# RWKV-7 recurrence and expert layer: another form of the first inverse, w turned on load, a new order

## The chip, the cores and the metric

The kernel runs on one core of a Trainium2 chip. Time is device microseconds of that core, as a median of several executions. The core has five engines that run their own instruction lists: TensorE (PE; loading its weights is listed apart, as PEld), VectorE (DVE), ScalarE (ACT), GpSimd (POOL) and SyncE (SP), which here only issues transfers. Matrix products go to PSUM, which this kernel splits into four double tiles ("duo").

## The reference

Two parts follow each other. The first is a recurrence over 768 steps for 4 x 8 heads with a 40 x 40 state each:

```
for t in range(S):
    y[t]  = r[t] @ state
    Sa    = state @ a[t]
    state = state * w[t][None, :] - outer(Sa, b[t]) + outer(v[t], k[t])
```

The second takes the 3072 x 320 result as x, and computes `gelu(x @ w_in) @ w_out` with a hidden width of 2048. w_in and w_out are given in double precision.

## The kernel before

**Chunks.** The 768 steps are cut into 12 chunks of 64. Inside a chunk, products of 64 x 64 blocks replace the steps; only the state goes from chunk to chunk. Heads and batches are packed so that one step of the kernel works on all 32 of them: a "run" is 32 calls of a small product, which the trace lists as 64 records.

**The steps.** The code is a set of generators; the name of each carries the chunk's number. For a chunk: `w`, `a`, `b`, `k`, `v`, `r` load rows; `logs` takes log w; `sums` makes running sums of it over time by products with the triangular matrix `cum_m`, once turned (heads on partitions, 32 products of 64x64) and once in rows (`cum`), and takes exponentials of them; `sc` and `sk` scale b and k; `ta`, `tb`, `tk`, `tv`, `tr` bring the inputs to turned form. From a certain chunk on (NT = 3 for a, v, r; NB = 4 for b, k) the turned form is not made by PE transposes but loaded a second time in pairs of rows (`bp`, `kp`, `vp`) and turned by VectorE (`turn`). `N`, `A`, `RV`, `M` are masked products of these. `av`, `X` and `sa` form the right-hand side and apply the inverse; `saT` is the same product turned, which `M` needs. `QY` gives the new state and y; `y` scales y into `xt` and moves parts of it between partitions with eleven transfers, on which the first product of the expert layer, `ph`, waits.

**The inverse.** Each chunk needs the inverse of a unit triangular 64 x 64 matrix per head and batch, T. From chunk 1 on, N goes to DRAM (`N`), comes back with blocks on partitions (`nb`), GpSimd solves (`inv`), and the result returns (`ft`); `corner` and `joined` fill the off-diagonal blocks. Chunk 0 has no time for that: `sq` builds its 32 x 32 diagonal inverses on PE by repeated squaring, five rounds in two halves, and `cornerd` and `joinedd` finish it.

**The expert layer.** `ph` (line 1002) is x times w_in, with Gelu on ScalarE (line 1005) evicting PSUM. `po` is the second product: direct for the first NS = 3 chunks and the last one (line 1024), otherwise by seven half-size products after Strassen and Winograd (line 1040), with additions on VectorE; the sums of w_out that these need (`ws`) lie in the tile that b and k of the first chunks leave. `wi`, `wl`, `wo` load w_in and w_out as 32-bit words, and `ci`, `co` convert them to single precision on VectorE and ScalarE. `warm` is a product that nothing uses.

**The order.** Nothing is scheduled by a tool. The string ORDER is a list of steps written out; each token runs a generator to its next yield, and `name:n` names the PSUM or conv buffers taken. Every engine, SyncE's transfer queue included, executes its instructions in that order. A line number in a profile of a product is often that of the helper `mm` (line 143).

## Time and profile before

| | |
|---|---|
| median of 3 runs | 685.69 us (685.41 to 689.18) |
| the profiled execution | 687.68 us |
| its span | 685.9 us, granted clock 0.992 |
| PE busy, PEld busy | 664.5 us (97%), 573.5 us (84%) |
| VectorE, ScalarE, GpSimd busy | 367.7, 216.9, 342.4 us |
| ph, PE (line 1002) | 219.0 us |
| po by half products, PE (line 1040) | 74.6 + 37.2 + 19.1 us |
| po direct, PE (line 1024) | 73.4 us |
| transfers, share of 16 engines | 54.2% on SyncE's queue |

A group's busy time is the union of its records; PE's products overlap, so the mean time of one record is longer than busy time by count.

### The profile page before, as it was taken

To read this page: it belongs to the slowest core of one execution; us is meant where nothing else is said; L and a number is where in the kernel's file an instruction comes from. 1 tells how busy PE (TensorE), PEld (TensorE's weight loads), DVE (VectorE), ACT (ScalarE), POOL (GpSimd) and SP (SyncE) were. 2 spreads that over 40 slices of the span, in tenths; PEclk is the share of its full clock that TensorE was granted. 3 is DMA by queue.
4 is the path that set the end of the run, shared out by engine and by line. 5 is a ranking of instruction groups with operands and counts; after the bars stand their busy time and mean duration, and the time that the engine had idled before them with its cause. 6 is when DMAs were issued, how large, how long until landed. Compare 5 with 4: busy or idle time off the path is not lost.

```text
span 685.9 us, 32624 instructions
## 1 busy us (share of the span) xinstructions
PE 664.5 (97%) x14748; PEld 573.5 (84%) x14748; DVE 367.7 (54%) x504; ACT 216.9 (32%) x300; POOL 342.4 (50%) x781
## 2 busy tenths in 40 slices
PE   8778999999999999999999999999999999999996
PEld 5665788788788778998998988988998998989984
DVE  1676878983533554845671853663744825613400
ACT  4243644524223312413423415322422412132010
POOL 3248406814837818826827827817816848700000
PEclk9899999999999999999999999999999999999999
DMA  9989377496479476556586377385656265210100
GB/s 133 181 158 160 68 162 178 125 177 120 88 135 149 88 141 116 106 103 127 102 147 113 78 145 135 62 171 111 113 109 129 52 116 104 40 37 4 39 1 20
DMA packets 287923, 74.46 MB, mean 109 GB/s; under 512 B 265736, under 2 KB 284456, under 8 KB 287784
## 3 DMA queue, kind: packets, MB, share of 16 engines
q1 hardware_dynamic: 286720, 69.84, 54.2%
q0 software_dynamic: 864, 2.36, 1.9%
q8 instruction: 116, 1.90, 1.2%
q14 instruction: 23, 0.19, 0.1%
q10 hardware_dynamic: 200, 0.16, 0.1%
HBM read 58.69 MB, written 9.70 MB: 100 GB/s over the span
## 4 chain that ended last, share of the span: by engine, by line
PE 92%; DVE 3%; issue 2%; SPq 1%; DMA 1%; ACT 0%; DVEq 0%; ACTq 0%
PE duo L1002 32%; PE duo L143 29%; PE duo L1040 18%; PE duo L1024 10%; PE duo L508 3%; SPq L207 1%; DMA xt<-in_b_dram 1%; DVE nT L565 0%; DVE conv L434 0%; DVE conv L440 0%; DVE aT L539 0%; DVE Nb L771 0%; DVE w_out_sb L441 0%; DVE N L627 0%; DVE SM L627 0%
## 5 line engine op out<-in xcount | busy, mean ns | idle before, releaser
L1002 PE MATMUL duo<-xt,w_in_sb 64*128 64x256 f32 x1920 | 219.0, 380 | 0.7 <-issue 0.6
L1002 PEld LDWEIGHTS duo<-xt,w_in_sb 64*128 64x128 f32 x1920 | 184.6, 187 | 22.1 <-issue 2.3
L730 POOL TENSOR_TENSOR tmp<-W,Nb 128x126 f32<-128x126 f32 (+22 forms) x310 | 132.6, 428 | 128.9 <-DMA Nb<-N 105.4
L732 POOL TENSOR_TENSOR W<-W,tmp 128x126 f32<-128x126 f32 (+22 forms) x310 | 135.5, 437 | 24.3
L1005 ACT ACTIVATE gt<-duo 128x1024 f32<-128x1024 f32 x48 | 49.2, 1024 | 173.3 <-PE duo L1002 165.8
L1040 PE MATMUL duo<-w_out_sb,gt 128*128 128x160 f32 x512 | 74.6, 302 | 0.0
L1024 PE MATMUL duo<-w_out_sb,gt 128*128 128x320 f32 x256 | 73.4, 438 | 1.0 <-DVE w_out_sb L441 1.0
L1040 PEld LDWEIGHTS duo<-w_out_sb,gt 128*128 128x128 f32 x512 | 70.2, 190 | 1.6 <-DVE os L1044 0.5
L1024 PEld LDWEIGHTS duo<-w_out_sb,gt 128*128 128x128 f32 x256 | 47.2, 190 | 20.9 <-DVE w_out_sb L441 1.6
L1040 PE MATMUL duo<-extra,conv 128*128 128x160 f32 x256 | 37.2, 303 | 0.0
L1040 PEld LDWEIGHTS duo<-extra,conv 128*128 128x128 f32 x256 | 35.0, 190 | 1.6 <-issue 1.0
L627 DVE TENSOR_TENSOR SM<-duo,upper 128x1024 f32<-128x1024 f32 x12 | 14.6, 1220 | 33.2 <-PE duo L143 33.2
L143 PE MATMUL duo<-rT,late 40*64 40x64 f32 x1536 | 27.6, 219 | 2.7 <-issue 2.4
L143 PEld LDWEIGHTS duo<-rT,late 40*64 40x64 f32 x1536 | 25.0, 135 | 4.7 <-issue 4.3
L854 DVE COPY Tt<-duo 32x512 f32<-32x512 f32 x11 | 7.6, 689 | 36.1 <-ACT Tt L854 36.0
L1044 DVE TENSOR_TENSOR os<-os,duo 128x160 f32<-128x160 f32 x32 | 10.1, 317 | 31.1 <-PE duo L1040 21.2
L723 POOL MEMSET W<- 128x512 f32 x10 | 5.5, 546 | 40.8 <-DMA inv<-W 40.7
L831 DVE STREAM_TRANSPOSE conv<-Tt 128x512 f32<-128x512 f32 x11 | 7.8, 711 | 32.2 <-DMA Tt<-inv 32.2
L730 POOL TENSOR_TENSOR rows<-os,rows 128x126 f32<-128x126 f32 (+22 forms) x31 | 13.5, 436 | 22.7 <-DMA rows<-N 20.4
L1005 ACT ACT_TABLE_LOAD x12 | 15.4, 1283 | 29.9 <-PE duo L1002 11.3
L945 DVE TENSOR_TENSOR xt<-duo,wpT 128x512 f32<-128x512 f32 x24 | 15.4, 682 | 17.0 <-PE duo L143 17.0
L429 ACT ACTIVATE conv<-conv,rebias 128x320 uint32<-128x320 uint32 (+1 forms) x26 | 15.8, 621 | 16.7 <-DVE conv L425 16.6
(194 smaller groups left out, 1034.0 us busy)
## 6 DMA issues: line engine op xcount, KB each, us to landing
Nb<-N SPq DMA_DIRECT2D x20, 256.0 KB
VR<-in_v_dram SPq DMA_DIRECT2D x24, 160.0 KB
out_dram<-os SPq DMA_DIRECT2D x48, 80.0 KB
rows<-in_b_dram SPq DMA_DIRECT2D x22, 160.0 KB
rows<-in_k_dram SPq DMA_DIRECT2D x22, 160.0 KB
Tt<-inv SPq DMA_DIRECT2D x44, 64.0 KB
r_pairs<-in_r_dram SPq DMA_DIRECT2D x36, 72.0 KB
a_pairs<-in_a_dram SPq DMA_DIRECT2D x18, 144.0 KB
```

Source lines behind the costliest of these rows:

```text
L143: nc.tensor.matmul(o, lhsT, rhs, start=first, stop=True, skip_group_check=True)
L429: nc.scalar.activation(power, power, ACT.Relu, bias=rebias, scale=8.0)
L508: nc.tensor.transpose(pt[:, g, n], src(g, n), ident)
L627: nc.vector.tensor_tensor(to, pt, upper.unsqueeze(1).to_broadcast([P, NBL, C]), ALU.mult)
L730: eng.tensor_tensor(t, W[:, :nr, j:j + 1].to_broadcast([P, nr, rest]), Nb[:, j:j + 1, j + 1:].to_broadcast([P, nr, rest]), ALU.mult)
L732: eng.tensor_tensor(W[:, :nr, j + 1:], W[:, :nr, j + 1:], t, ALU.add)
L945: nc.vector.tensor_tensor(xt[:, :NP, g * P:(g + 1) * P].rearrange("p i (e t) -> p i e t", e=2), t["QY"][g][:, :, :, D:].rearrange("p e i t ...
L1002: nc.tensor.matmul(pt[:, x, s], w_in_sb[half(x), kt, p * P:(p + 1) * P], xt[half(x), kt], start=kt == 0, stop=kt == NK - 1)
L1005: nc.scalar.activation(gt[:, 4 * q:4 * q + 4].rearrange("p (x s) t -> p x s t", x=2), pt, ACT.Gelu)
L1024: nc.tensor.matmul(pt[:, g], gt[:, f, g * P:(g + 1) * P], w_out_sb[:, f], start=f == 0, stop=f == NF - 1)
L1040: nc.tensor.matmul(pt[:, n, :DM // 2], l_[:, f], r_[:, f], start=f == 0, stop=f == NF // 2 - 1)
L1044: nc.vector.tensor_tensor(to, one_, other, ALU.add)
```

## The change

- The inverse of chunk 0 works with one 64 x 64 block-diagonal product per head and batch and half (64 x 96 with the running result beside it) in place of two of 32 x 32. The mask that cuts the blocks out is a new constant.
- For chunk 0, `av` multiplies A by V and by the masked r-v part together, and `sa` applies T to both, so M comes out of sa's product under a mask (`left_upper`); `saT` and `M` of chunk 0 are gone.
- For chunks 3 to 11, w is loaded a second time in pairs (`wq`), turned by VectorE, and its running sums over time are made there by a scan (`wt`) in place of PE's products in `sums`.
- b and k are turned by VectorE from chunk 3 on (before: 4), and po uses half products from chunk 2 on (before: 3).
- w_in comes in 2 steps in place of 4, w_out in 11 transfers in place of 32, with more bytes in each; the hidden columns are permuted to suit.
- `warm` is one product in place of two, and there are nine of them in place of six.
- ORDER is new throughout, and has other buffer places. The second copy of the inverse's corner (T2) is read in place.

```diff
+FIRST = (3, 3, 3, 2)
-    NT, NB, NS = 3, 4, 3
+    NT, NB, NW, NS = FIRST
...
+    def wq(c):
+        fetch_pairs("w_turned", w, c, paired["v"], False)
+        yield
...
+    left_upper = sb("left_upper", [P, VC])
+    upper = left_upper[:, D:]
+    upper_blocks, ident_block = plain(Js_tile)[:, :C], plain(Js_tile)[:, C:C + BL]
+    going_on = sb("going_on", [P, G * NP * 2 * C], mybir.dt.uint8)
...
     def wo(c):
+        n = 2 if c in SECOND_PAIRS else 1
         src = moe_w_out.bitcast(UINT32) if wide_out else moe_w_out
-        for n in range(2):
-            nc.sync.dma_start(out=to[:, n::2], in_=from_[:, n::2])
+        at = (c // 2 % 2 * (NF // 2) + 2 * (c // 4) + c % 2) * P
+        nc.sync.dma_start(out=second_words(c, n).rearrange("p (f m) -> p f m", f=n),
+                          in_=src[at:at + n * P].rearrange("(f p) m -> p f m", p=P))
...
     def sums(c):
+        if c < NW:
+            pt = duo().rearrange("p e (n t) -> p e n t", t=C)
+            for n in range(G * NP):
+                for x in range(2):
+                    for e in range(2):
+                        at = (2 * n + x) * D
+                        mm(pt[half(x), e, n], logw[half(e), at:at + HP], cum_m[half(e), half(e)])
+            yield
...
+    def wt(c):
+        logs_of = conv()[:, :G * NP * P].rearrange("p (n t) -> p n t", t=C)
+        turn(logs_of, c, "w_turned")
+        yield
+        nc.scalar.activation(plain(logs_of), plain(logs_of), ACT.Ln)
+        yield
+        nc.vector.tensor_tensor_scan(plain(logs_of), going_on, plain(logs_of), 0.0, ALU.mult, ALU.add)
+        yield
+        en = of(c)["en"] = by_batch(kT_tile)
+        nc.scalar.activation(plain(en), plain(logs_of), ACT.Exp, scale=-1.0)
+        wp = of(c)["wp"] = wps[c % 2]
+        nc.scalar.activation(wp.rearrange("p (n e) t -> p e n t", e=2)[:, :, :, 1:],
+                             logs_of.rearrange("p (e n) t -> p e n t", e=2), ACT.Exp)
...
     def av(c):
+        if c == 0:
+            for x in range(2):
+                pt = duo()[:, :, :NP * VC].rearrange("p g (i d) -> p g i d", i=NP)
+                for i in range(NP):
+                    for g in range(G):
+                        for e in range(2):
+                            mm(pt[half(e ^ x), g, i], t["A"][half(e), x, g, i],
+                               VRs[0][half(e), g, i // NA, 2 * (i % NA) + x])
+                yield
+                nc.scalar.copy(first_av[x].rearrange("p (g i) d -> p g i d", g=G), pt)
+                yield
+            return
...
     def sq(c):
+        nc.vector.transpose(ZT[:, ns], Z_blocks[:, ns])
+        yield
+        nc.vector.tensor_tensor(T[:, ns], Z[:, ns, :BL], Z[:, ns, BL:C], ALU.add)
+        nc.vector.tensor_tensor(T[:, ns], T[:, ns], ident_block.unsqueeze(1).to_broadcast([P, NBL // 2, BL]), ALU.add)
         yield
         for k_ in range(5):
             last = k_ == 4
+            cols = slice(C if last else 0, C + BL if k_ else C)
+            for n in range(NBL // 4):
+                for z in range(2):
+                    f = ns.start + z * NBL // 4 + n
+                    for q in range(2):
+                        mm(pt[half(q), z, n, cols], ZT[half(q), f], Z[half(q), f, cols])
+            yield
             if not last:
+                nc.vector.transpose(by_duo(ZT), pt[:, :, :, :C])
                 yield
             if k_:
+                nc.vector.tensor_tensor(by_duo(T), by_duo(T), pt[:, :, :, C:], ALU.add)
                 yield
+            if not last:
+                nc.scalar.copy(by_duo(Z_blocks), pt[:, :, :, :C])
+                yield
...
     def sa(c):
+        if c == 0:
+            for x in range(2):
+                ...
+                            mm(pt[half(e), g, i], Tt_tile[half(e ^ x), x, g, i], first_av[x][half(e ^ x), g * NP + i])
+                yield
+                for g in range(G):
+                    nc.vector.tensor_tensor(SM[:, g].rearrange("p q (a x) c -> p x (q a) c", x=2)[:, x], pt[:, g],
+                                            left_upper.unsqueeze(1).to_broadcast([P, NP, VC]), ALU.mult)
+                yield
+            return
...
     def warm(c):
-        pt = duo()
-        for n in range(2):
-            mm(pt[:, n], ident, cum_m.unsqueeze(1).to_broadcast([P, 4, P]))
+        mm(duo()[:, 0], ident, cum_m.unsqueeze(1).to_broadcast([P, 4, P]))
```

## The prediction

> **What bounds the kernel now.** I read the page first: engine shares, then the chain that ended last. Two lines of the page:

> ```profile
> PE 664.5 (97%) x14748; PEld 573.5 (84%) x14748; DVE 367.7 (54%) x504; ACT 216.9 (32%) x300; POOL 342.4 (50%) x781
> ...
> PE 92%; DVE 3%; issue 2%; SPq 1%; DMA 1%; ACT 0%; DVEq 0%; ACTq 0%
> ```

> The matrix engine is busy nearly all the time and 92% of the chain is its own work. An average hides stages, so next the windows view, cut at the first ph (88 us), ahead of VectorE's first turns of chunk 3 (140) and at the last but one ph (601); columns are PE, PEld, DVE, ACT, POOL busy, granted clock, DMA share, GB/s:

> ```profile
> 0.00:88.00 88.00, 75.09 (x2130) 56.06 (x2130) 54.11 (x89) 38.02 (x52) 39.27 (x106) 0.94 0.79 140
> 88.00:140.00 52.00, 50.67 (x1006) 42.95 (x1008) 43.63 (x82) 25.20 (x34) 26.67 (x64) 1.00 0.68 155
> 140.00:601.00 461.00, 459.56 (x10534) 406.33 (x10534) 253.39 (x310) 139.50 (x196) 276.51 (x611) 1.00 0.61 114
> ```

> From 140 to 601 PE idles 1.4 us of 461: there, PE time removed is time gained unless something new makes it wait. Up to 88 us it idles 12.9 us and also runs fillers (warm). There the first chunk's chain counts: inverse, sa, M, QY, y, transfers, first ph. Its timeline, PE rows:

> ```profile
> 60.56 0.85 PE L143 MATMUL duo<-Tt,avs 64*64 64x64 f32 x41 [0.44 <-issue]
> ...
> 65.66 0.92 PE L143 MATMUL duo<-rT,late 40*64 40x64 f32 x45 [2.43 <-issue]
> 66.51 3.68 PE L143 MATMUL duo<-cum_m,ident 128*128 128x512 f32 x4
> 70.12 1.66 PE L143 MATMUL duo<-SM,extra 64*64 64x104 f32 x64
> ```

> Between saT0 and QY0 lie 10.6 us (59.56 to 70.12), 2.43 of them an issue wait and 3.68 a filler that takes 1.98 elsewhere. Last, the transfer queue of SyncE, which the page doesn't show as busy:

> ```profile
> 312.01 6.30 SPq L218 DMA_DIRECT2D r_pairs<-in_r_dram  x8
> 318.35 4.84 SPq L218 DMA_DIRECT2D v_pairs<-in_v_dram  x8
> 323.29 2.74 SPq L233 DMA_DIRECT2D w_tile<-in_w_dram  x4
> 326.09 1.36 SPq L1014 DMA_DIRECT2D out_dram<-os  x2
> 327.54 2.20 SPq L221 DMA_DIRECT2D a_pairs<-in_b_dram  x4
> ```

> Its rows stand back to back: of 300 to 400 us, 85.6 are issue rows. Summed over the whole timeline, the 756 issues take 516.7 us, 0.683 each, with a median gap of 0.044; I price one at 0.727. It is the nearest second bound.

> **What comes off the path after the first ph.** PE is full there, so I count marginal PE time from the chain (a run of 64 small products 1.01 us, from "2.02 PE duo L143 x128"; eight 128x128 turns 0.92, from 2.77 for 24).
> 1. Running sums of w turned, chunks 3 to 11: nine runs of 64 go, 9 x 1.01 = 9.1 us.
> 2. Chunk 3 turns b and k on VectorE: two runs of eight, 1.85 us. Its row sums become four products of half height, 0.72 in place of 1.34: 0.6 us.
> 3. Chunk 2's second product by seven half products: 64 records of 128x320 at 0.281 (4.50 for 16) are 18.0; 112 of 128x160 at 0.142 (4.54 for 32) are 15.9: 2.1 us.

> Sum 13.6 us; its least is 0, if all of it turns into waits.

> **What these steps load elsewhere.** Turned w puts on VectorE, per chunk, a transpose (1.24) and a scan. No row shows a scan: from below a 1024 tensor_tensor, 1.22; from above two passes of the 1024 scalar_tensor_tensor, 2.81; nearest is one such pass, two operations an element, 1.40. Nine chunks: 24 us (22 to 36). Chunk 3's b and k add 1.24 x 2 + 1.40 + 1.23 = 5.1, chunk 2's sums four of 1.3 and seven small (19.2 / 8 = 2.4), 7.6. VectorE rises from 368 to some 404, 60% of a shorter run: off the path, covered by 40% idle.

> [...]

> ScalarE loses four half exponentials a chunk (2.41) and gains a logarithm and two exponentials of 1024 (some 3.1), and the order has 46 table loads for 36: 10 x 1.283 + 9 x 0.7 = 19 us, 217 to 236. Queued behind the exponentials, which wait for the scan, are the Gelu evictions that give PE its PSUM tiles back. Their cover: ScalarE waits 165.8 us over 37 times for PE in front of them, 4.5 each. If that is gone, a load per added set costs 12.8 in all.

> SyncE: turned w adds four issues a chunk (36), chunk 3's b, k, w ten; larger loads of w_in and w_out take 37 away, nearly all before chunk 3. By count, 756 become 765. Up to the last transfer of the first y, 83 issues for 95. From there to that of chunk 10, 655 for 638: 17 x 0.727 = 12.4 us more. The queue had 49.7 us without issues in that stretch (513.5 - 638 x 0.727). PE needs 513.5 - 13.6 = 500 there, SyncE 655 x 0.727 = 476: it still fits, with 24 us to spare. I take 0, bounds 0 to 26.

> **The start.** Chain of chunk 0, in three pieces.
> 1. The a load is issued behind both b loads, two issues later: 0 to +1 us.
> 2. Inverse. Ten half rounds, in two alternating halves. A round was: 64 products (half of 1.68 for 128, 0.84), transpose 0.45, copy 0.37, add 0.42: 2.1 us; five are 10.4, and took 27.5 (19.6 to 47.1), since PE waited for issue (1.92, 0.44, 1.64), VectorE did masks and w_in words in between and the clock was 0.83 in 20 to 40 us. A round becomes 32 products of 64x96 (between 64x64, 0.58, and 64x104, 0.83; I take 0.83, the nearer width), transpose of 512 columns 0.71, add 0.42, copy 0.59: 2.55, so +2.4 over five. Half as many PE records (320 for 640) mean fewer fetch waits: up to -4.0. I take -1, bounds -4 to +2.4. The four narrow adds (1.68) at a half's begin become two (0.84).
> 3. From sa to QY. saT0, its two copies, M0 and its mask go; sa0 is two runs of 32 at 0.83 with four masking multiplies (between 320 columns, 0.48, and 512, 0.68: 0.6), the last two behind the last run, and one filler of half size: 0.83 x 2 + 1.2 + 0.95 = 3.8 for 10.6, -6.8; without the issue wait and the slow filler, which may come again, -2.7. I take -5. The wider av0 costs 0.5 (1.66 - 1.14).

> Behind QY0 nothing is shorter: 3.1 of products, 1.3 of y, eleven transfers (75.2 to 83.8). PE's own work ahead of the first ph falls by some 4 (saT0, M0, three half fillers), so it doesn't hold the gain up. Start: +0.5 - 1 - 5 + 0.5 - 0.8 = -5.8, bounds -11 to +1. Tail (last PE record near 680.2, end 685.9): unchanged; two table loads after the last copy, 2.6 us, lie under the stores.

> **Sum.** -13.6 - 5.8 = -19.4. The profiled execution took 687.68 (span 685.9); the median of three, 685.69, is 2.0 below it. 687.68 - 19.4 = 668.3 for such an execution, and 666 for the median.

> **Rivals.**
> - The start gains nothing (a round of the inverse is longer by itself, and the waits come again): 672. For it: five rounds of 2.1 took 27.5, so waits rule; against: saT0 and M0 are gone for certain.
> - ScalarE holds PSUM back: ten more table loads, 12.8, on the path: 679. For it: Exp waits for a scan behind a transfer, in front of Gelu; against: the 4.5 us per Gelu.
> - The PE time isn't a bound, so the 13.6 turn into waits: 680. PEld has 406 of 461 us in the long window. Against: a ph record takes 380 ns and its load 187, and PE idles 1.4. [...]
> - The other side: SyncE sets the pace. The 12.4 us of added issues come on top, and its 50 us without issues stay, because they are waits for work that y and N deliver: from the first y's transfers to chunk 10's takes 525.8, with the start at -5.8 and the remaining 88.7 as before: 78.0 + 525.8 + 88.7 = 692.5 of span, 692 for the median. It decides once more than 24 of those 50 us stay. For it: only 1.2 us of wait ahead of the y transfers of chunks 0, 1 and 6; against: 12.6, 6.1 and 3.3 us ahead of those of chunks 10, 9 and 7.
> - Better: start at its bound, 658.

> **How the numbers follow.** Forecast 0.50 (660 to 671), start without gain 0.14, ScalarE 0.10, PE not the bound 0.04, SyncE 0.14, better 0.08. 0.5% is 3.4 us, about what a measurement can tell here. Faster: all but SyncE's case and 0.02 of the tails of ScalarE's and PE's, 0.84; within it, 0.05; slower, 0.11. The range 657 to 685 leaves out the upper part of SyncE's case, 0.11, and a few of the better ones.

> **What would show it.** Right: PE idle in the long window still under 5 us; no run of 64 from w_tile after chunk 2; first ph at 80 to 84; saT and M rows 11, not 12; last PE record near 661. Wrong: waits of PE for y's transfers or of SyncE rows back to back ahead of y (SyncE's case); waits for Gelu with table loads in front (ScalarE's); rounds of the inverse over 5.5 us (start).

## The result: no gain, 0.75% slower

The changed kernel takes 691.45 us (median of 20 runs) where the kernel before took 685.79 in the same session (20 runs). The ratio of the means is 1.0075, with a 95% interval of 1.005 to 1.0099; it leaves out one execution of the changed kernel, 697.43 us, which was slower than the rest. The forecast was 666, in a range of 657 to 685: wrong in sign and outside the range.

The page of the changed kernel, the same two lines as before (engines: busy time, share, instructions; then the chain that ended last by engine):

```profile
PE 659.5 (96%) x13754; PEld 573.0 (83%) x13754; DVE 408.1 (59%) x533; ACT 241.1 (35%) x304; POOL 376.4 (55%) x791
...
PE 77%; DVE 8%; POOL 5%; DMA 3%; issue 3%; ACT 2%; SPq 2%; DVEq 0%; ACTq 0%
```

TensorE does 994 instructions fewer, yet its busy time fell by 5.0 us only, and its share of the chain from 92% to 77%. VectorE (408, forecast 404) and ScalarE (241, forecast 236) grew as the counts said. GpSimd grew by 34 us, which no step of the prediction held. The windows, with the same cuts (columns: PE, PEld, DVE, ACT, POOL busy, granted clock, DMA share, GB/s):

```profile
0.00:88.00 88.00, 73.07 (x1400) 55.85 (x1400) 48.06 (x80) 35.44 (x46) 39.76 (x108) 0.88 0.86 150
88.00:140.00 52.00, 48.89 (x1089) 40.69 (x1088) 46.60 (x81) 24.11 (x34) 29.95 (x65) 0.97 0.76 149
140.00:601.00 461.00, 454.97 (x10018) 405.81 (x10020) 293.25 (x348) 161.13 (x200) 298.65 (x600) 1.00 0.66 122
```

Two places differ. Up to 88 us the clock is 0.88 in place of 0.94; and from 140 to 601 PE idles 6.0 us in place of 1.4, while GpSimd is busy for 22 us more. In the profiled executions the first ph starts at 96.60 us (before 87.89): the start lost 8.7 us. From there to the end of the span it is 592.6 us (before 598.0): 5.4 gained of the 13.6 forecast. Together the span is 3.3 us longer where 19.4 less were forecast. Of the 22.7 us between the two, 14.5 lie in the start and 8.2 behind the first ph.

**The start.** The PE timeline of the changed kernel at the points that the prediction named:

```profile
24.76 1.13 PE L146 MATMUL duo<-w_in_sb,Nb 64*64 64x64 f32 x32
...
34.43 0.70 PE L146 MATMUL duo<-aT,kT 40*64 40x64 f32 x13 [4.31 <-issue]
35.05 2.07 PE L146 MATMUL duo<-cum_m,ident 128*128 128x512 f32 x2
37.06 4.73 PE L146 MATMUL duo<-w_in_sb,Nb 64*64 64x96 f32 x64
...
59.94 3.30 PE L146 MATMUL duo<-w_in_sb,Nb 64*64 64x32 f32 x58 [3.74 <-issue]
...
76.56 1.38 PE L146 MATMUL duo<-N,Tt 64*64 64x104 f32 x26
...
80.32 1.67 PE L146 MATMUL duo<-SM,extra 64*64 64x104 f32 x64
```

From these rows and those of before:

| stretch | before | after | difference |
|---|---|---|---|
| to the inverse's first product | 20.43 | 24.76 | +4.3 |
| from there to sa0 (before: saT0) | 39.1 | 51.8 | +12.7 |
| from there to QY0 | 10.6 | 3.8 | -6.8 |
| from there to the first ph | 17.8 | 16.3 | -1.5 |
| sum, the first ph | 87.89 | 96.60 | +8.7 |

From sa to QY takes the 3.8 us that the prediction added up. What comes ahead of it ate the gain. Twice PE has a wait that the profile lists as "issue", with nothing it can name behind it (4.31 and 3.74 us, the longest was 2.43 before), and beside each wait the granted clock falls to 0.5, for 6.8 and 13.7 us: 64 products of 64x96 take 4.73 at 37.06 us in place of some 3 (32 of them took 1.50 at 45.78). In all 20.5 us before the first ph ran at half the clock, against 10.2 before the change.

The trace's packets tell what these waits are for. Each of them ends 1.4 to 1.5 us after a 16 KB block of the instruction queue has landed, and the other issue waits of this trace end 1.3 to 1.6 us after one. The two blocks took 1.4 us, which is within what blocks take here (0.9 to 1.8), but they began only at 31.5 and 57.2 us, when PE had been idle since 30.1 and 56.2. At both places a large load of w_in is in transit: its packets of 4 KB run from 20.1 to 32.0 and from 50.1 to 61.6 us. What holds a block back until then the trace doesn't show.

The clock also halved behind shorter waits, for 3.4 us each time: of 1.2 to 2.4 us before the change (at 22.3, 32.5 and 66.6 us), and of 1.4 and 1.1 us behind the first ph of the changed kernel (at 109.2 and 208.2 us).

**After the first ph.** Which group's instructions grew on GpSimd (line, engine, operation, shapes; busy us, mean ns; idle before); before the change, then after:

```profile
L732 POOL TENSOR_TENSOR W<-W,tmp 128x126 f32<-128x126 f32 (+22 forms) x310 | 135.5, 437 | 24.3
L730 POOL TENSOR_TENSOR tmp<-W,Nb 128x126 f32<-128x126 f32 (+22 forms) x310 | 132.6, 428 | 128.9 <-DMA Nb<-N 105.4
```

```profile
L781 POOL TENSOR_TENSOR W<-W,tmp 128x126 f32<-128x126 f32 (+22 forms) x310 | 148.8, 480 | 24.3
L779 POOL TENSOR_TENSOR tmp<-W,Nb 128x126 f32<-128x126 f32 (+22 forms) x310 | 147.1, 474 | 92.2 <-DMA Nb<-N 68.7
```

The same 620 instructions of the inverses of chunks 2 to 11 take 27.8 us more. PE's two largest waits from 90 to 680 us (engine, line, waited for: us in total, times, longest), after the change:

```profile
PE duo L146 <- issue: 3.9, 5, 1.4
PE duo L146 <- DVE conv L888: 2.6, 2, 1.4
```

Line 888 is the transposition with which corner starts on the returned inverse. So the inverse comes late, but the largest part is waits for instructions, of which there were 0.9 us before.

### The profile page after: what moved, and what is told of

Same layout as the page of the kernel before. It is cut to its first block, busy times and chain, and to the rows that moved or that the text cites. A ratio compares the mean times of both kernels' runs of the same rounds, so it can differ in the third digit from the quotient of the medians.

```text
span 689.2 us, 30712 instructions
## 1 busy us (share of the span) xinstructions
PE 659.5 (96%) x13754; PEld 573.0 (83%) x13754; DVE 408.1 (59%) x533; ACT 241.1 (35%) x304; POOL 376.4 (55%) x791
## 4 chain that ended last, share of the span: by engine, by line
PE 77%; DVE 8%; POOL 5%; DMA 3%; issue 3%; ACT 2%; SPq 2%; DVEq 0%; ACTq 0%
PE duo L146 26%; PE duo L1072 26%; PE duo L1110 16%; PE duo L1094 6%; POOL W L781 2%; POOL tmp L779 2%; PE duo L540 2%; DMA Tt<-inv 1%; DVE conv L455 1%; DMA Nb<-N 1%; DVE conv L449 1%; DVE aT L571 1%; DVE conv L527 1%; DMA inv<-W 1%; DMA v_pairs<-in_w_dram 1%
## 5 line engine op out<-in xcount | busy, mean ns | idle before, releaser
L1072 PE MATMUL duo<-xt,w_in_sb 64*128 64x256 f32 x1920 | 223.1, 385 | 0.2 <-DVE VR L659 0.2
L779 POOL TENSOR_TENSOR tmp<-W,Nb 128x126 f32<-128x126 f32 (+22 forms) x310 | 147.1, 474 | 92.2 <-DMA Nb<-N 68.7
L781 POOL TENSOR_TENSOR W<-W,tmp 128x126 f32<-128x126 f32 (+22 forms) x310 | 148.8, 480 | 24.3
L1110 PE MATMUL duo<-w_out_sb,gt 128*128 128x160 f32 x576 | 84.2, 303 | 0.1
L1094 PE MATMUL duo<-w_out_sb,gt 128*128 128x320 f32 x192 | 53.9, 436 | 0.0
L1094 PEld LDWEIGHTS duo<-w_out_sb,gt 128*128 128x128 f32 x192 | 35.7, 190 | 14.6 <-issue 0.5
L1110 PE MATMUL duo<-extra,conv 128*128 128x160 f32 x288 | 41.9, 302 | 0.3 <-issue 0.3
L588 POOL TENSOR_TENSOR rows<-rows,w_tile 128x640 f32<-128x640 f32 x9 | 15.5, 1723 | 46.7 <-ACT w_tile L505 21.7
L1110 PEld LDWEIGHTS duo<-extra,conv 128*128 128x128 f32 x288 | 39.5, 190 | 1.2 <-issue 0.4
L779 POOL TENSOR_TENSOR rows<-os,rows 128x126 f32<-128x126 f32 (+22 forms) x31 | 14.5, 469 | 27.8 <-DMA rows<-N 25.5
L544 DVE STREAM_TRANSPOSE late<-v_pairs 128x1024 f32<-128x1024 f32 x9 | 11.2, 1243 | 19.6 <-DMA r_pairs<-in_r_dram 9.4
L527 DVE TENSOR_TENSOR_SCAN conv<-going_on,conv 128x1024 f32<-128x1024 uint8 x9 | 21.6, 2402 | 1.1 <-ACT conv L525 1.1
```

What stands on the lines that cost most here:

```text
L527: nc.vector.tensor_tensor_scan(plain(logs_of), going_on, plain(logs_of), 0.0, ALU.mult, ALU.add)
L544: nc.vector.transpose(to.rearrange("p n (s y) -> p n y s", y=2), raws.pop((c, n)).rearrange("p n (y d) -> p n y d", y=2)[:, :, :, :BL])
L588: (nc.gpsimd if c in SCALED_BY_POOL or c >= NB else nc.vector).tensor_tensor(to, raws.pop((c, "k")), t["rw"], ALU.mult)
L779: eng.tensor_tensor(t, W[:, :nr, j:j + 1].to_broadcast([P, nr, rest]), Nb[:, j:j + 1, j + 1:].to_broadcast([P, nr, rest]), ALU.mult)
L781: eng.tensor_tensor(W[:, :nr, j + 1:], W[:, :nr, j + 1:], t, ALU.add)
L1072: nc.tensor.matmul(pt[:, x, s], w_in_sb[half(x), kt, p * P:(p + 1) * P], xt[half(x), kt], start=kt == 0, stop=kt == NK - 1)
```

## The experiments

Times are medians; ratios are to the kernel before on the same chip, with 95% intervals. The experiments ran on five chips, so two of them are compared by their ratios, and a difference is then known to some 3 to 4 us. "Idle" is PE's time without a record between the first ph and its last product: 2.8 us before, 9.0 in the changed kernel. "On e1" means that the edit is made to the version e1, not to the changed kernel.

### What the start loses

Theory: the large loads of w_in (four of 768 KB or 1 MB with rows of 4 KB, where the kernel before has sixteen of 192 or 256 KB with rows of 1 KB) delay the transfers that bring PE's instructions; PE idles and the clock halves. Rivals: the fillers, which are half as long; the new inverse itself.

**e1, w_in in pieces of 1 KB**, the size of before:

```diff
-            nc.sync.dma_start(out=words[half(x), :n], in_=src[...].rearrange("(i r) n -> r i n", i=n)[:HP])
+            whole = src[...].rearrange("(i r) n -> r i n", i=n)
+            for m in range(0, wd, 256):
+                nc.sync.dma_start(out=words[half(x), :n, m:m + 256], in_=whole[:HP, :, m:m + 256])
```

> The changed kernel with one thing undone: the two large loads of w_in per step are issued in four pieces of 256 words (1 KB) a row, as before the change. Theory 1 (blocks of PE's instructions arrive late behind the 4 KB rows of the w_in loads; the long idle then halves PE's clock): longest issue wait of PE before 88 us falls from 4.31 to 2.5 or less, half clock before the first ph from 20.5 us to some 10, first ph from 96.6 to about 90, time about 685 (ratio to before 0.999). Rival 2 (the start is late because a round of the new inverse is longer and the new order leaves PE waiting for VectorE and ScalarE): first ph stays at 95 to 97, time 691 (ratio 1.008).

Measured: 684.60 us, ratio 0.9967 (0.9934 to 0.9999). The first ph starts at 87.0, half clock before it falls to 6.8 us. PE's issue waits from 10 to 100 us, in the changed kernel and then in e1:

```profile
PE duo L146 <- issue: 9.1, 5, 4.3
```

```profile
PE duo L146 <- issue: 3.3, 1, 3.3
```

The first wait shrinks from 4.31 to 3.25 us (2.5 was expected), the second is gone. The pieces alone bring the first ph 9.6 us forward in the profiled executions, more than the 8.7 lost; by the ratios they are worth 7.4 us in all, give or take 3. e1 and the eleven versions built on it that keep its loads have the first ph at 87.0 to 89.6 us, the three with large loads at 92.9 to 99.6. But what follows the first ph went up by 4.9 us, to 597.5, and idle from 9.0 to 14.5 us: with the start mended all but 0.5 us of the gain behind it is gone. The windows from 140 to 601 show PE less busy than in the changed kernel:

```profile
140.00:601.00 461.00, 449.69 (x9944) 401.89 (x9942) 283.73 (x330) 151.84 (x189) 301.48 (x610) 1.00 0.64 119
```

**e3, pieces of 512 B**

```diff
-            for m in range(0, wd, 256):
-                nc.sync.dma_start(out=words[half(x), :n, m:m + 256], in_=whole[:HP, :, m:m + 256])
+            for m in range(0, wd, 128):
+                nc.sync.dma_start(out=words[half(x), :n, m:m + 128], in_=whole[:HP, :, m:m + 128])
```

> As the first, with pieces of 128 words (512 B): one size changed. Theory 1: longest issue wait of PE before 88 us 1.5 or less, half clock less than with 1 KB, time 683 to 686, unless the 24 more issues on SyncE's queue hold up the later loads. Rival 2: 691 or more.

Measured: 687.64 us, 1.0021 (0.9992 to 1.005), above the 683 to 686 expected. No wait for instructions is over 1.6 us, but once PE waits 5.7 us for a copy of the inverse on ScalarE; half clock before the first ph is 10.2 us and the first ph at 91.4. Smaller is not better.

**e8, the kernel before with its w_in loads joined** (8 loads of 512 words a row in place of 16 of 256):

```diff
-            for m in range(0, wd // 2, 2 * P):
-                nc.sync.dma_start(out=words[half(x), :n, m:m + 2 * P], in_=whole[:HP, :, m:m + 2 * P])
+            nc.sync.dma_start(out=words[half(x), :n], in_=whole[:HP])
```

> The kernel before with one part of the change alone: each w_in load of 256 words a row is joined with its neighbour to 512 words (2 KB), 8 loads in place of 16. Theory 1: longest issue wait rises from 2.43 to 3 or more, first ph from 87.9 to 89 to 92, time 687 to 690 (ratio 1.002 to 1.006). Rival 2: the loads are harmless, 685.8, or a little less since SyncE has eight issues fewer.

Measured: 691.62 us, 1.0069 (1.0044 to 1.0094). The first ph moves from 87.9 to 92.6 and half clock before it from 10.2 to 20.5 us; behind it little changes (599.8 us for 598.0). So larger loads alone cost 4.7 us, with none of the rest of the change. How they do it is only in part as expected: issue waits up to 100 us rise from 8.5 to 10.1 us, but the longest from 2.4 to 2.5 only, not to 3 or more.

**e2, fillers of two products** (the size of before)

```diff
-        mm(duo()[:, 0], ident, cum_m.unsqueeze(1).to_broadcast([P, 4, P]))
+        pt = duo()
+        for n in range(2):
+            mm(pt[:, n], ident, cum_m.unsqueeze(1).to_broadcast([P, 4, P]))
```

> The changed kernel with fillers of two products in place of one, as before the change. Theory 1: the issue waits of 4.31 and 3.74 us stay, half clock before the first ph stays over 14 us, time 689 to 692. Rival 3 (the halved fillers let the clock fall): half clock before the first ph 10 us or less, first ph at 90 or earlier, time 685.

Measured: 699.60 us, 1.0149 (1.01 to 1.0198); half clock before the first ph 17.1 us, first ph at 99.6. The two waits stay (4.1 and 3.8 us), so the halved fillers aren't the cause. The time is above the 689 to 692 expected: of 8.8 us more span 5.8 lie behind the first ph, for which no reason was found.

**f4, no fillers**, on e1:

```diff
     def warm(c):
-        mm(duo()[:, 0], ident, cum_m.unsqueeze(1).to_broadcast([P, 4, P]))
         yield
```

> The changed kernel with 1 KB pieces of w_in (684.6 us), and the nine fillers left out, 8.5 us of PE time in the start. If they are there for the clock and it needs them: more half clock than 6.8 us ahead of the first ph, first ph at 88 to 93, and 686 to 690. If the clock drops by the waits for instructions alone: first ph at 83 to 87 and 680 to 684.

Measured: 685.95 us, 0.9981 (0.9948 to 1.0013), first ph at 89.6, half clock 13.7 us before it, in place of 6.8. The fillers keep the clock up to some degree and cost about what they gain; they explain neither loss.

### What eats the gain after the first ph

Theory: VectorE's scan over w holds GpSimd, so the inverses come late. Rivals: SyncE's queue; PE is not the bound.

**f1, no scan**, on e1:

```diff
-        nc.vector.tensor_tensor_scan(plain(logs_of), going_on, plain(logs_of), 0.0, ALU.mult, ALU.add)
```

> The changed kernel with 1 KB pieces of w_in (684.6 us; PE idle 14.5 us after the first ph), and the VectorE scan of chunks 3 to 11 left out: the running sums of w of these chunks are not made, so the exponentials take the logarithms themselves, and what comes out is not the reference's recurrence. Everything else issues as it did. Theory (the scan, 2.40 us on VectorE, holds one GpSimd instruction for some 2.2 us each time and makes the way to the next N longer, so the loop from N by GpSimd's inverse to the corner is what PE waits for): PE's idle time after the first ph falls from 14.5 to under 6 us, GpSimd's busy time by about 16, and the time to about 676. Rival (the added loads of w on SyncE's queue, or other waits, set the pace): 683 to 685, with the idle time where it was.

Measured: 678.41 us, 0.9879 (0.9843 to 0.9915); idle 7.2 us, GpSimd 20 us less busy (378.1 to 358.0). That is 6.0 us by the ratios, give or take 3.4, and a little short of the 676 us and 6 us of idle time expected. The chain that ended last, in e1 and then without the scan:

```profile
PE 46%; POOL 19%; DMA 11%; SPq 9%; DVE 7%; issue 5%; ACT 1%; DVEq 0%; ACTq 0%; POOLq 0%
```

```profile
PE 80%; SPq 10%; DMA 5%; DVE 3%; issue 1%; ACT 1%; DVEq 0%; ACTq 0%
```

In e1 more than half of the chain runs outside PE, over GpSimd's inverse and the transfers around it; without the scan GpSimd is gone from it. PE's waits from 90 to 680 us, the issue waits and those for corner, in e1 and then without the scan:

```profile
PE duo L146 <- issue: 6.3, 7, 2.0
PE duo L146 <- DVE conv L889: 3.5, 6, 1.0
```

```profile
PE duo L146 <- issue: 5.2, 6, 1.5
PE duo L146 <- DVE conv L888: 0.7, 1, 0.7
```

The waits for the inverse go with the scan; those for instructions stay.

**g4, two transposes in place of the scan**, on e1, as long on VectorE (2 x 1.24 for 2.38 us):

```diff
-        nc.vector.tensor_tensor_scan(plain(logs_of), going_on, plain(logs_of), 0.0, ALU.mult, ALU.add)
+        for n in range(2):
+            nc.vector.transpose(plain(logs_of), plain(logs_of))
```

> The changed kernel with 1 KB pieces of w_in (684.6 us), and in place of the scan of chunks 3 to 11 two 32x32 transposes of the same 128x1024 tile, 1.24 us each: VectorE is as long busy, but GpSimd's instructions are never stretched beside transposes in these traces, and beside the scan each time. The running sums of these chunks are not made. If the scan costs because it holds GpSimd: as without the scan, 677 to 680, and GpSimd's busy time some 16 to 20 us less. If it costs by its length on VectorE: 683 to 686.

Measured: 679.88 us, 0.9897 (0.9851 to 0.9944), GpSimd's busy time as without a scan. So most of the scan's 6 us, 4.8 by the difference of the ratios (give or take 3.9), is what it does to GpSimd and not its time on VectorE; from the version without a scan this one can't be told. How that looks, in the timelines of e1, GpSimd and then VectorE:

```profile
281.70 0.42 POOL L782 TENSOR_TENSOR W<-W,tmp 128x121 f32<-128x121 f32 x1
282.19 2.25 POOL L780 TENSOR_TENSOR tmp<-W,Nb 128x110 f32<-128x110 f32 x1
```

```profile
281.95 2.31 DVE L528 TENSOR_TENSOR_SCAN conv<-going_on,conv 128x1024 f32<-128x1024 uint8 x1
```

An instruction that takes 0.4 us takes 2.25, and ends 0.2 us behind the scan. That is so beside each of the nine scans (2.1 to 2.3 us in the changed kernel); GpSimd's other long instructions (there 0.8 to 1.5 us) lie beside VectorE operations with two inputs in SBUF, such as the additions of the half products, of which chunk 2 now has a set more.

**f2, w's second load issued twice**, on e1:

```diff
-        fetch_pairs("w_turned", w, c, paired["v"], False)
+        for n in range(2):
+            fetch_pairs("w_turned", w, c, paired["v"], False)
```

> The changed kernel with 1 KB pieces of w_in (684.6 us), and the second load of w in chunks 3 to 11 issued twice: 36 issues more on SyncE, some 0.69 us each, 25 us of its queue. If SyncE's queue sets the pace (the rival of the prediction, 692 us): 15 to 25 us more, 700 to 710. If PE waits for GpSimd's inverse and SyncE still has room: 0 to 5 us more, 684 to 690.

Measured: 700.43 us, 1.0195 (1.0159 to 1.0232): 15.8 us for 36 issues. By itself this is what SyncE's rival said, so the opposite was tried.

**g1, w's second load left out in chunks 4 to 11**, on e1:

```diff
-        fetch_pairs("w_turned", w, c, paired["v"], False)
+        if c == NW:
+            fetch_pairs("w_turned", w, c, paired["v"], False)
+        raws[c, "w_turned"] = paired["v"]
...
-        nc.scalar.activation(plain(logs_of), plain(logs_of), ACT.Ln)
+        nc.scalar.activation(plain(logs_of), plain(logs_of), ACT.Ln, scale=1.0 if c == NW else 0.0, bias=0.0 if c == NW else 1.0)
```

> The changed kernel with 1 KB pieces of w_in (684.6 us), and the second load of w left out in chunks 4 to 11: 32 issues less on SyncE, some 22 us of its queue. What is turned is then whatever the tile holds, its logarithm is taken as that of one, and the recurrence of these chunks has no decay. The turn, the scan and the exponentials stay. If SyncE's queue is one of the two things that are late (the doubled load cost 15.8 us): 672 to 679, with PE's idle time after the first ph under 9 us. If it only began to be late with the doubled load: 682 to 686.

Measured: 683.39 us, 0.9972 (0.9939 to 1.0004), against 684.60 and 0.9967 with the loads: nothing that can be told apart, to some 3 us. SyncE's queue doesn't set the pace as the kernel stands; it has little room left, and another 25 us of issues are past it. In f2 the largest PE waits that are new are for v's load and for y's transfers:

```profile
PE duo L146 <- DMA VR<-in_v_dram: 2.9, 2, 2.8
PE duo L1074 <- DMA xt<-xt: 2.7, 2, 1.9
```

**f3, PE time put back**: a product of 128x512 that nothing uses in each of chunks 3 to 11, on e1.

```diff
-        cum = duo()[:, :, :DM]
+        cum = duo()
+        if c >= NW:
+            mm(cum[:, 0], ident, cum_m.unsqueeze(1).to_broadcast([P, 4, P]))
+        cum = cum[:, :, :DM]
```

> The changed kernel with 1 KB pieces of w_in (684.6 us), and one 128x512 product that nothing uses put back ahead of the row sums of w in chunks 3 to 11, which is about the PE time that the turned sums took (9 of some 0.95 us, 8.6 us). If PE's time is still worth its length: 693. If PE's waits for the inverse take it up: 685 to 688, with the idle time after the first ph falling from 14.5 to 6 to 9 us.

Measured: 687.94 us, 1.0025 (0.9999 to 1.0051), idle 6.3 us. Of 8.6 us of added PE time 4.0 show in the end by the ratios, give or take 2.9, and idle falls by 8.2. Read backwards: with the scan in the way, taking these products out gains less than half of their length.

**f5, k's scaling on VectorE** from chunk 4 on (before: GpSimd), on e1:

```diff
-        (nc.gpsimd if c in SCALED_BY_POOL or c >= NB else nc.vector).tensor_tensor(to, raws.pop((c, "k")), t["rw"], ALU.mult)
+        (nc.gpsimd if c in SCALED_BY_POOL else nc.vector).tensor_tensor(to, raws.pop((c, "k")), t["rw"], ALU.mult)
```

> The changed kernel with 1 KB pieces of w_in (684.6 us), and the scaling of k in the chunks from 4 on taken by VectorE in place of GpSimd. If GpSimd is what is late (its inverse is stretched and starts behind other work): its busy time falls by 10 us or more, PE's idle time after the first ph from 14.5 to 7 to 10, and the time to 677 to 681. If VectorE, which then has some 10 us more, is late itself: no gain or a loss, 684 to 690.

Measured: 693.93 us, 1.0112 (1.0072 to 1.0152): worse than either expectation, though GpSimd is 14.6 us less busy. Idle stays at 14.2 us. One wait of 3.8 us at 191.7, for an operation of VectorE (nT, line 598), is followed by 10.2 us of half clock, so PE waits for VectorE there; and the moved operation has two inputs in SBUF as well. What made VectorE late was not followed further.

**g2, w's second load issued by ScalarE**, on e1:

```diff
-        fetch_pairs("w_turned", w, c, paired["v"], False)
+        fetch_pairs("w_turned", w, c, paired["v"], False, nc.scalar)
...
-                    nc.sync.dma_start(out=to, in_=pairs[rows_, :, cols])
+                    by.dma_start(out=to, in_=pairs[rows_, :, cols])
```

> The changed kernel with 1 KB pieces of w_in (684.6 us), and the second load of w of chunks 3 to 11 issued by ScalarE in place of SyncE. If SyncE's queue is late: 676 to 682. If not, or if ScalarE is held by the wait for the tile ahead of Gelu: 684 to 695.

Measured: 699.51 us, 1.0193 (1.015 to 1.0236), above both expectations; idle 21.9 us, one PE wait of 6 us ahead of a ph. There a Gelu stands behind the load's issues on ScalarE, which is idle for 8.15 us up to 281.0.

### A scan that doesn't hold GpSimd

The scan's inputs both lie in SBUF. In the traces of before and after, each instruction of GpSimd's inverses over 0.8 us (41 and 64 of 682) overlaps a VectorE operation with two inputs in SBUF; those that overlap only other VectorE operations, which read PSUM or have one input, take 0.51 us at most. If the two inputs in SBUF are the reason, one input in PSUM frees GpSimd.

**h1, the scan reads PSUM in seven chunks**, on e1 (in ORDER the second `wt` step of chunks 4, 5, 6, 7, 8, 10 and 11 gets a PSUM place, and moves behind `av3`, `RV4`, `tn5` and `A7` in chunks 4, 5, 6 and 8):

```diff
-        nc.scalar.activation(plain(logs_of), plain(logs_of), ACT.Ln)
+        logs = duo().rearrange("p e t -> p (e t)") if places else plain(logs_of)
+        nc.scalar.activation(logs, plain(logs_of), ACT.Ln)
         yield
-        nc.vector.tensor_tensor_scan(plain(logs_of), going_on, plain(logs_of), 0.0, ALU.mult, ALU.add)
+        nc.vector.tensor_tensor_scan(plain(logs_of), going_on, logs, 0.0, ALU.mult, ALU.add)
```

> The changed kernel with 1 KB pieces of w_in (684.6 us), and in seven of the nine chunks from 3 on (all but 3 and 9) the logarithm of w goes to a PSUM tile that is free at that point of the order, and the scan reads it there. In chunks 4, 5, 6 and 8 the logarithm is taken a few steps later for that. The result stays the reference's. If the scan holds GpSimd because both of its inputs lie in SBUF: GpSimd's stretched instructions beside the scan fall from nine to two, and 678 to 681. If a scan holds GpSimd wherever its inputs lie, or if PE waits for the PSUM tile: 683 to 688.

Measured: 690.23 us, 1.0044 (1.0014 to 1.0074), above both expectations. The timelines of GpSimd, VectorE and PE around one such scan:

```profile
334.04 0.39 POOL L783 TENSOR_TENSOR W<-W,tmp 128x96 f32<-128x96 f32 x1
334.51 0.36 POOL L781 TENSOR_TENSOR tmp<-W,Nb 128x91 f32<-128x91 f32 x1
334.94 0.36 POOL L783 TENSOR_TENSOR W<-W,tmp 128x91 f32<-128x91 f32 x1
```

```profile
333.87 2.29 DVE L529 TENSOR_TENSOR_SCAN conv<-going_on,duo 128x1024 f32<-128x1024 uint8 x1
```

```profile
336.21 1.14 PE L146 MATMUL duo<-st,aT 40*64 40x40 f32 x64 [3.43 <-DVE conv L529]
```

The reason stands: the scan takes as long (2.29 us), GpSimd runs beside it at 0.36 to 0.39, only the two scans left in SBUF stretch an instruction, and GpSimd's busy time falls to 355 us. But the gain doesn't come. Idle is 14.9 us, about as in e1 (14.5), and 5.8 of it are now three waits of PE for the PSUM tile that the scan reads:

```profile
PE duo L146 <- DVE conv L529: 5.8, 3, 3.4
```

**h2, the same with the changed kernel's own loads of w_in** (against h1):

```diff
-            for m in range(0, wd, 256):
-                nc.sync.dma_start(out=words[half(x), :n, m:m + 256], in_=whole[:HP, :, m:m + 256])
+            nc.sync.dma_start(out=words[half(x), :n], in_=whole[:HP])
```

> The changed kernel with the scan reading from PSUM in seven of nine chunks, but with its own large loads of w_in. If the two losses add up: 691 less some 5, 685 to 688, with the first ph at 95 to 98. If the late start hides the waits for the inverse (PE waited 9.0 us after the first ph in the changed kernel, 14.5 with the start mended): 688 to 691.

Measured: 696.02 us, 1.011 (1.0064 to 1.0155): above both of its expectations, with the same waits for the tile (5.9 us in three), 13.7 us of half clock before the first ph and 10.2 behind it. It says nothing on whether the two losses add up.

**h3 and h4, PSUM in five chunks (4, 6, 8, 10, 11) and in three (4, 10, 11)**. In ORDER, h3 against h1, and h4 does the same for 6 and 8:

```diff
-wt5:0 QY3 v4 RV4 wt5:3 po2:1 po2 wt5
+wt5:0 wt5 QY3 v4 RV4 po2:1 po2 wt5
...
-wt7:0 y5 w7 po4:2 wt7:2 wt7
+wt7:0 y5 w7 po4:2 wt7 wt7
```

> The changed kernel with 1 KB pieces of w_in (684.6 us), and the scan reading from PSUM in chunks 4, 6, 8, 10 and 11 alone; in chunks 5 and 7, where PE waited 1.6 and 3.4 us for the PSUM tile, it reads SBUF again. If the loss of the version with seven came from these waits of PE: 679 to 683. If the way by PSUM costs in itself what it saves on GpSimd: 684 to 689.

> As above with chunks 4, 10 and 11 alone, where the tile taken is free the longest. Three of nine scans off GpSimd are worth some 2 us by the run without scans (6.2 for nine): 682 to 684. If the way by PSUM costs in itself: 684 to 687.

Measured: 685.07 us, 0.9971 (0.9949 to 0.9994), and 683.99 us, 0.9961 (0.9936 to 0.9985), with idle of 11.6 and 9.5 us. The loss of h1 is gone with chunks 5 and 7, but a gain over e1 (0.9967) can't be told: h3 missed the 679 to 683 expected, and h4 lies where both of its expectations meet. By f1 five and three scans off GpSimd should be worth 3 and 2 us, about what these runs can resolve; whether the way by PSUM costs that much in itself stays open. e1, h3 and h4 are the fastest versions that leave nothing out: 0.3 to 0.4% under the kernel before, 1.0 to 1.1% under the changed one, by the loads of w_in.

## Why the prediction was wrong

Two steps failed. The larger is the start: -5.8 us forecast, +8.7 measured. The other is the price of nothing for what VectorE took over: 13.6 us forecast behind the first ph, 5.4 measured, and 0.5 in e1.

- **PE's own work.** Right. The three terms made 13.6 us. From the first ph on, the span without PE's idle time is 595.2 us before, 583.6 after, 583.0 in e1 and 580.7 without the scan: 11.6 to 14.5 less, the smaller ones with two and one stretches of 3.4 us at half clock in them.
- **"Its least is 0, if all of it turns into waits".** That is nearly the case that came. The step that failed is the price of VectorE's added work: 36 us "off the path, covered by 40% idle", priced at nothing. VectorE's own time was about right: 40 us were added, and a scan, for which the sum took 1.40, measured 2.40, inside its bounds. What was left out is that an instruction on VectorE made one of another engine longer (0.4 us became 2.25 beside a scan). The trace of before had it: 41 instructions of GpSimd's inverses took over 0.8 us (0.90 to 1.65), and lay beside additions of the half products and other VectorE work with two SBUF inputs. GpSimd's 342 us were read and never put into the sum. The scan costs some 6 us of the 13.6 by f1. The waits that remain without it (7.2 us for 2.8) account for another 4.4; 5.2 of the 7.2 are issue waits, where before there were 0.9. Why instructions come late more often there stays open.
- **The start, -5.8.** It lost 8.7. From sa to QY gave -6.8 where -5 was taken: right. Two terms failed. The inverse, "-1, bounds -4 to +2.4", measured +12.7 up to sa0; with smaller loads alone it is +2.9 (e1). The reasoning was that half as many PE records mean fewer waits for instructions. Up to 100 us there are 5 for 6, but they take 9.1 us for 8.5, and the half clock comes on top. The larger loads of w_in were counted only among 37 issues fewer. The piece ahead of it, "0 to +1 us", measured +4.3, and +4.5 in e1, so it is not the loads'. The inputs are 1.4 us later; the inverse's first transposition ends at 21.6 us (before 20.3), and its first product stands until 24.8 behind turns and chunk 1's product in the new order. That this place in the order is the cause was not tried, nor what makes the inverse 2.9 longer in e1.
- **"The start gains nothing", 672.** Its sign came: from the inverse's first product to the end of the last round (24.76 to 63.24) a round takes 7.7 us, against the 5.5 named. That waits come again was right; that they do no more than cancel the gain was not.
- **SyncE, "I take 0, bounds 0 to 26".** The 0 holds (g1). Its rival, 692 us, has the measured time almost to the microsecond by luck, and is wrong as a cause: PE's list of waits has none for y's transfers, and without the added loads the time stays; its reading of the queue as nearly full is right (f2). By single records an issue of before takes 0.676 us and not 0.683, which changes nothing in the sum.
- **ScalarE's table loads, 679.** Nothing for it: from 90 us on, the changed kernel has no wait of PE for ScalarE among those listed.
- **PE not the bound, 680.** Half of it came: more than half of the 13.6 us turned into waits. Its reason, weight loads, did not. In the long window weight loads are as busy as before (405.8 of 461 us) while PE waits for corner and for instructions, so the loads are not what took the place of products.
- The signs named ahead: the first ph at 80 to 84 and an idle time under 5 us were missed (96.6 and 6.0), and so was a last PE record near 661 (683.6 is where it ends); no run from w_tile after chunk 2 and one M row fewer came true.

## What to carry to other kernels

Before pricing work that is moved to an idle engine at nothing, look at which instructions of other engines become long beside that kind of work in the trace at hand: the price is paid there, and by whoever waits for them. A load that is made larger to save issues can cost more than they do: in the start here, where TensorE already waited for its instructions, larger loads alone (e8) took these waits from 8.5 to 10.1 us, the half clock from 10.2 to 20.5 us and the first ph back by 4.7 us. And a gain counted in TensorE time is only worth its length as long as the next loop, here N to GpSimd to corner, keeps the slack that it had (in f3, 4.0 of 8.6 us).
